# Soft-MoE over thresholded attention on one core: 28 weight blocks are issued pair by pair behind the loads of q, and GpSimd's scaling of k is planned later

## The chip, the cores and the metric

The kernel runs on one core of a Trainium2 chip. A core has five engines with a queue each, which run their instructions in order and wait for each other through semaphores: TensorE (PE in the profile; its weight loads are PEld), VectorE (DVE), ScalarE (ACT), GpSimd (POOL) and SyncE (SP), which here only issues DMA transfers. PE writes to PSUM, GpSimd works on SBUF alone. The metric is the time of one execution on the device in microseconds (us), the median of several runs.

## The reference, cut to what matters

```python
scores = q @ k.T / sqrt(64)                      # 8 batches x 8 heads, 576 x 576, head size 64
thresh = scores.max(-1) - tau
scores = where(scores >= thresh, scores, -1e9)
attn   = softmax(scores);  x = attn @ v          # x: 4608 rows x 512 (all heads of a row side by side)
logits = x @ phi                                 # 32 slots, 4 for each of 8 experts
d = softmax of logits over the 4608 rows;  slot_input = d.T @ x
for e in range(8):                               # w1[e]: 512 x 1024, w2[e]: 1024 x 512
    slot_out[e] = relu(slot_input[e] @ w1[e]) @ w2[e]
out = (softmax of logits over the 32 slots) @ slot_out
```

All of it is computed in 32-bit floats. The weights w1 and w2 are 32 MB; they are needed only after the last attention row is there, since `slot_input` sums over all rows.

## The kernel before, in words

**Pairs.** The attention runs over 32 pairs of heads, `NP` = 8 batches x 4 (`pair(p)`, line 448). A pair loads its k (two transfers, L468), its q (two transfers, one for each head's 64 partitions, L473) and its v (one, L480). Two buffers each for k, q and v are there, so a pair's k and q can be loaded only when the pair before the last has made all its scores, and v when that pair has multiplied by its v. The k is first multiplied by a flag over 8 (L475): by VectorE in halves for the first pair, by GpSimd in one instruction of 128 x 576 for every other.

A pair has nine tiles of scores, each 128 x 576: both heads' rows against their keys. For each tile PE makes the scores (L494, the ninth L499), VectorE takes the maximum of a row (L504, `nmx`), ScalarE the exponential (L512), GpSimd works out the threshold (L515, `thr`), and VectorE masks and sums (L518). GpSimd adds a small number to the sums (L525, `ri`), VectorE takes the reciprocal (L528), and GpSimd normalises the tile, called `p` or `pL` (L532). Then PE transposes (L420), ScalarE copies the transposes out of PSUM (L425 and L564; `pTa`, `pTb`, `pTl`), PE multiplies by v (L579) and transposes back. After each fourth pair the batch's logits, its running softmax over rows and its share of `slot_input` are made (`dispatch`, line 622).

PSUM holds four regions, each for one tile of scores or a set of transposes. The tail after the last pair (lines 810 to 971) runs the experts and the combination.

**The weights.** The 64 blocks of 512 KB (a block is 128 x 1024) are fetched by `load_unit` (L397; the transfer for w1 is L404, for w2 L406). The first `NPRE` = 28 go to buffers of their own, which are free from the beginning; 19 more, called `host`, go after the last loads of the attention into room that the attention gives back, and the last 17 in the tail.

**The order of the work** is made while the program is built, by a list planner (`Order`, line 99). `G.add(engine, duration, number, function, reads, writes, after)` registers an operation. `plan` (line 150) walks through a modelled time: an operation becomes ready when all it depends on has ended, plus a latency of the engine it comes from, `LAT` (or `SAME` where the same engine follows). A free engine takes, among the ready operations that find a buffer, the one with the lowest number. The numbers are in steps, nine to a pair, and most are replaced by those in `TABLE` (lines 34 to 79), which are kept by pair and by the operation's place in it. `after` adds a dependence for the planner alone. The planned times set the order in each engine's queue and the buffers, nothing else; on the chip each instruction then waits for the data and buffers that it needs. For a transfer SP's `LAT` is the time that the planner allows from the end of the issue to the landing.

In the table the loads of k and GpSimd's scaling of k have low numbers (39 and 19 steps ahead of their pair), so that each is taken as soon as it is ready.

For the changed lines: in `pair`, the loads and the scaling; after the loop over the pairs, the loop that registers the 28 blocks, with numbers 8, 12, 16 and so on up to 116 and no dependence:

```python
for i in range(NPRE):
    G.scope("load", 4 * (i + 2))
    G.add("SP", 1460, 4 * (i + 2), lambda i=i: load_unit(wslots[i]))
```

Of the kernel before, what the change touches and what calls it, by code (L numbers as in the profile page):

```python
# [14 lines left out]
AX = mybir.AxisListType  # L15
PSUM = bass.MemoryType.PSUM

LAT = {"PE": 197, "DVE": 140, "ACT": 152, "POOL": 160, "SP": 2400}
SAME = {"PE": 0, "DVE": 127, "ACT": 143, "POOL": 0, "SP": 2100}
SLOTS = dict(  # L20
    k=2, q=2, vv=2, r=3, ri=3, nmx=4, thr=4, p2=4, pL=1, pTa=1, pTb=1, pTl=1, l4=1,
# [77 lines left out]
class Order:  # L99
# [50 lines left out]
    def plan(self, table):  # L150
# [49 lines left out]
        while ev:  # L200
# [10 lines left out]
            for eng in engs:  # L211
# [26 lines left out]
                heapq.heappush(ev, (end, 2, -1))  # L238
                heapq.heappush(ev, (end + LAT[eng], 0, got))
                for j in succ[got]:  # L240
                    left[j] -= 1
                    lat = (SAME if ops[j][0] == eng else LAT)[eng]
                    rdy[j] = max(rdy[j], end + lat)
# [24 lines left out]
def softmax_attention_soft_moe(  # L268
# [17 lines left out]
    nc = tc.nc  # L286
    B, HP, D, _, S = qT.shape
    NP = B * HP
    N9 = 9
# [87 lines left out]
    G = Order(kinds)  # L377
# [10 lines left out]
    wslots = [wp.tile([128, 1024], F32, name=f"w{i}") for i in range(NPRE)]  # L388
# [3 lines left out]
    n = NPRE + NHOST  # L392
# [4 lines left out]
    def load_unit(t):  # L397

        if len(where) == len(units):
            return  # L400
        i, kind, _, e, k = units[len(where)]
        where[i] = t
        if kind == 0:
            nc.sync.dma_start(t, w1[e, k * 128:(k + 1) * 128, :])  # L404
        else:
            nc.sync.dma_start(t, w2[e, k * 256:(k + 1) * 256, :].rearrange("(p j) f -> p (j f)", j=2))  # L406
# [41 lines left out]
    def pair(p):  # L448
        b, j = divmod(p, HP)
        t0 = p * N9  # L450
        G.scope("first" if p == 0 else "last" if p == NP - 1 else "pair", t0)
        kt, qt, vv = (Buf(k) for k in ("k", "q", "vv"))
# [5 lines left out]
        def pool(dur, nom, fn, r, w):  # L458
            G.add("POOL", dur, nom, fn, r, w)
# [4 lines left out]
        for hs in parts:  # L464
            kc, n = slice(hs[0] * HS, (hs[-1] + 1) * HS), len(hs)
            def keys(a=hs[0], z=hs[-1] + 1):
                for g in range(2):
                    nc.sync.dma_start(  # L468
                        kt.t[rows[g]].rearrange("p (h k) -> p h k", h=2)[:, a:z],
                        kT[b, j, :, 0:2 * S].rearrange("d (h g k) -> d g h k", h=2, g=2)[:, g, a:z])  # L470
            G.add("SP", 1200, t0 - 18 + hs[0], keys, w=[kt[h] for h in hs])
            for g in range(2):
                G.add("SP", 500 * n, t0 - 18 + hs[0], lambda g=g, a=hs[0], z=hs[-1] + 1: nc.sync.dma_start(  # L473
                    qt.t[rows[g], a:z], qT[b, j, :, a:z]), w=[qt[h, g] for h in hs])
            sc = lambda e, kc=kc: lambda: e.tensor_scalar(out=kt.t[:, kc], in0=kt.t[:, kc], scalar1=flag8, **one)  # L475
            if p == 0:
                G.add("DVE", 370, t0 - 9 + hs[0], sc(nc.vector), [], [kt[h] for h in hs])
            else:
                pool(730, t0 - 9, sc(nc.gpsimd), [], [kt[h] for h in hs])
        G.add("SP", 1100, t0 - 12, lambda: nc.sync.dma_start(vv.t, vt[b, j]), w=[vv], after=vload[-1:])  # L480
        vload.append(len(G.ops) - 1)

        p2s = {}
        for i in range(N9):
            t = t0 + i
            s, nmx, thr = Buf("s"), Buf("nmx"), Buf("thr")
            c, h = divmod(i, 2)
# [44 lines left out]
            if i < 8 and h == 1:  # L534
                w = Buf("s")
# [8 lines left out]
            if i == 3:  # L544
                w = Buf("s")
# [7 lines left out]
            if i == 8:  # L553


                w = Buf("s")
# [12 lines left out]
        for a, (pT, q) in enumerate(((pTa, slice(0, QA)), (pTb, slice(QA, S)))):  # L569
            n0 = u + OFF['a1' if a else 'a0']  # L570
            w = Buf("w")
            n = q.stop - q.start
# [12 lines left out]
        w = Buf("s")  # L585
# [148 lines left out]
    def csoft(rows):  # L734
# [7 lines left out]
        def guard():  # L742
# [10 lines left out]
    G.scope("load", 0)  # L753
    G.add("SP", 200, -12, lambda: nc.sync.dma_start(phi_sb, phi.rearrange("(j p) s -> p j s", p=128)),
          w=[PERS["phi"]])
    recent, last, vload = [], [], []
    for p in range(NP):
        recent.append(len(G.ops))
        pair(p)
        if p % HP == HP - 1:  # L760
            dispatch(p // HP)
    for i in range(NPRE):
        G.scope("load", 4 * (i + 2))
        G.add("SP", 1460, 4 * (i + 2), lambda i=i: load_unit(wslots[i]))

    G.scope("soft", NP * N9)
    for eng, n, fn in csoft(slice(0, row(B - 1))):
# [30 lines left out]
    for i in range(NHOST):  # L798
        n = next(n for n in range(NL) if sum(x[1] for x in sides[:n + 1]) >= (i + 1) * 4096)
        G.add("SP", 1350, NP * N9 + 9, lambda n=n, i=i: host(NL - 1 - n, i),  # L800
              after=sorted(set(sum(users[:n + 1], []))))
# [217 lines left out]
```

## Time and profile before

| what | value |
|---|---|
| median of three runs | 618.53 us (618.26 to 618.58) |
| the profiled execution | 613.17 us, of which 611.4 us span from the first to the last instruction |
| mean granted TensorE clock of the profiled execution | 0.977 |
| busy share of the span | PE 90%, VectorE 80%, ScalarE 72%, GpSimd 57% |
| moved by DMA | 82.98 MB, mean 136 GB/s |
| weight blocks (`w<-in_w`) | 45 of 512 KB, median 9.4 us from issue to landing |

How to read it: the profile is of one execution. A row of a timeline has the start and the length in us, the engine, the line of the kernel, the operation, what it writes and reads, the shape and how many were merged; in square brackets stand the idle time of the engine just before it and what ended that. A `q` behind an engine's name marks its queue's own instructions, such as the issue of a transfer. A row of a group has the busy time, the mean length in nanoseconds, and behind the second bar the idle time before the group and what ended most of it. A row of a table by stage has the busy time of each engine with its number of instructions, then the granted clock, the share of the 16 DMA engines that was busy, and GB/s. The issues are listed with their number, the size and the median us to landing. Idle time before an instruction that "ended" with an engine means that this engine's signal was the last that came.

The median of the runs is 5.36 us above the profiled execution.

### The profile page before, as it was taken

The page shows a single profiled execution, that of the slowest core. Times are in us where ns is not written, and L with a number is a line of the kernel's source. Part 1 is how long each engine was busy: PE and PEld are TensorE (multiplying, and loading weights), DVE is VectorE, ACT ScalarE, POOL GpSimd, SP SyncE. Part 2 cuts the span into 40 slices and gives each one's busy share as a digit, 9 for nine tenths or more (in the row PEclk, how much of TensorE's full clock was granted, in tenths as well). Part 3 has the DMA queues.
Part 4 walks back from the last instruction along what each step waited for, and adds up shares of the span by engine and source line. Part 5 has one row for each costly group of instructions (what it writes and reads, how often), then busy time and mean ns, then how long its engine had stood idle before and what let it go on. Part 6 is the DMA issues. An engine that isn't in the chain of part 4 may idle for free.

```text
span 611.4 us, 17335 instructions
## 1 busy us (share of the span) xinstructions
PE 547.4 (90%) x6342; PEld 332.8 (54%) x6342; DVE 487.1 (80%) x1146; ACT 442.5 (72%) x751; POOL 350.5 (57%) x799
## 2 busy tenths in 40 slices
PE   7799899999999999998999899899999998889991
PEld 5455555555555555555555555555565555443361
DVE  5689888898998988998898888898989999341182
ACT  3588878788888888888878788788788888512071
POOL 2666666666666765666656665676667746311030
PEclk9599999999999999999999999999999999989997
DMA  7989943133322332333333232233223321799578
GB/s 194 271 273 342 317 109 83 36 84 83 85 71 62 88 80 64 83 81 80 82 81 81 81 81 67 61 81 82 70 69 82 80 60 58 265 359 374 209 297 322
DMA packets 31989, 82.98 MB, mean 136 GB/s; under 512 B 4640, under 2 KB 12832, under 8 KB 31904
## 3 DMA queue, kind: packets, MB, share of 16 engines
q1 hardware_dynamic: 31904, 81.87, 43.9%
q8 instruction: 50, 0.82, 0.6%
q14 instruction: 35, 0.29, 0.2%
HBM read 72.42 MB, written 9.44 MB: 134 GB/s over the span
## 4 chain that ended last, share of the span: by engine, by line
PE 54%; ACT 16%; DVE 13%; issue 10%; POOL 3%; DMA 1%; DVEq 0%; SPq 0%; POOLq 0%; ACTq 0%
PE ps L579 18%; PE ps L494 13%; PE ps L420 10%; ACT p L512 8%; DVE p L518 6%; DVE nmx L504 4%; PE ps L499 3%; PE h L857 3%; ACT pTa L425 2%; PE so L887 2%; ACT pTl L425 2%; POOL p L532 2%; ACT pTb L425 1%; PE o L922 1%; PE ps L713 1%
## 5 line engine op out<-in xcount | busy, mean ns | idle before, releaser
L504 DVE TENSOR_REDUCE nmx<-ps 128x1 f32<-128x576 f32 x288 | 205.3, 752 | 33.4 <-PE ps L494 29.5
L518 DVE SCALAR_TENSOR_TENSOR p<-ps,thr,p 128x576 f32<-128x576 f32 x256 | 199.8, 812 | 9.2 <-POOL thr L515 7.7
L512 ACT ACTIVATE p<-ps,nmx 128x576 f32<-128x576 f32 x256 | 183.4, 746 | 30.3 <-DVE nmx L504 25.8
L532 POOL TENSOR_SCALAR p<-p,ri 128x576 f32<-128x576 f32 x256 | 189.4, 745 | 11.1 <-PE ps L420 3.1
L494 PE MATMUL ps<-k,q 64*128 64x288 f32 x1024 | 171.8, 438 | 6.7 <-issue 3.0
L420 PE MATMUL ps<-ident,p 64*128 64x64 f32 x2304 | 110.1, 229 | 24.8 <-ACT pTl L425 9.2
L420 PEld LDWEIGHTS ps<-ident,p 64*128 64x128 f32 x2304 | 90.9, 140 | 57.7 <-DVE p L518 15.5
L494 PEld LDWEIGHTS ps<-k,q 64*128 64x128 f32 x1024 | 86.8, 190 | 40.5 <-ACT pTb L425 11.4
L515 POOL TENSOR_SCALAR thr<-nmx,nabs 128x1 f32<-128x1 f32 x288 | 75.7, 268 | 34.0 <-DVE nmx L504 28.1
L525 POOL TENSOR_SCALAR ri<-r 128x2 f32<-128x2 f32 (+1 forms) x160 | 30.9, 193 | 98.7 <-DVE ri L528 43.5
L425 ACT COPY pTb<-ps 128x1024 f32<-128x1024 f32 (+1 forms) x95 | 80.8, 878 | 2.3 <-PE ps L420 1.3
L579 PE MATMUL ps<-pTb,vv 128*64 128x320 f32 x512 | 75.9, 438 | 0.3
L425 ACT COPY pTa<-ps 128x1024 f32<-128x1024 f32 x64 | 65.4, 1024 | 11.7 <-PE ps L420 11.0
L579 PE MATMUL ps<-pTa,vv 128*64 128x256 f32 x512 | 62.6, 387 | 0.0
L425 ACT COPY xT<-ps 128x256 f32<-128x256 f32 (+1 forms) x63 | 25.2, 400 | 51.1 <-PE ps L579 51.1
L579 PEld LDWEIGHTS ps<-pTb,vv 128*64 128x64 f32 x512 | 34.0, 136 | 37.1 <-ACT pTb L425 11.4
L579 PEld LDWEIGHTS ps<-pTa,vv 128*64 128x64 f32 x512 | 34.1, 137 | 26.3 <-ACT pTa L425 11.5
L475 POOL TENSOR_SCALAR k<-k,flag 128x576 f32<-128x576 f32 x31 | 23.0, 743 | 34.8 <-DMA k<-in_kT 21.2
L579 PE MATMUL ps<-pTl,vv 128*64 128x256 f32 (+1 forms) x256 | 41.9, 406 | 0.0
L528 DVE RECIPROCAL ri<-ri 128x2 f32<-128x2 f32 (+1 forms) x160 | 25.8, 161 | 15.1 <-POOL ri L525 15.0
L822 POOL TENSOR_TENSOR c<-lall,crow 128x512 f32<-128x512 f32 x9 | 9.3, 1045 | 46.8 <-PE ct L412 42.2
L425 ACT COPY pTl<-ps 128x256 f32<-128x256 f32 x64 | 23.7, 371 | 11.6 <-DVE p L518 7.8
(119 smaller groups left out, 485.4 us busy)
## 6 DMA issues: line engine op xcount, KB each, us to landing
w<-in_w SPq DMA_DIRECT2D x45, 512.0 KB, 9.4
q<-in_qT SPq DMA_DIRECT2D x62, 288.0 KB, 4.6
vv<-in_vt SPq DMA_DIRECT2D x32, 320.0 KB, 3.0
host<-in_w SPq DMA_DIRECT2D x19, 512.0 KB, 6.0
k<-in_kT SPq DMA_DIRECT2D x62, 144.0 KB, 3.1
out<-w SPq DMA_DIRECT2D x11, 512.0 KB, 5.6
out<-host SPq DMA_DIRECT2D x5, 512.0 KB, 6.4
out<-host SPq DMA_DIRECT2D x4, 256.0 KB, 4.9
```

The lines of the kernel that those rows point to most:

```text
L420: nc.tensor.transpose(out=s[:, g, c:c + 64], in_=ins[g], identity=ident[rows[g], rows[g]], tile_position=(64 * g, 0))
L425: G.add("ACT", 51 + 0.833 * n, nom, lambda: nc.scalar.copy(*io()), r, w)
L475: sc = lambda e, kc=kc: lambda: e.tensor_scalar(out=kt.t[:, kc], in0=kt.t[:, kc], scalar1=flag8, **one)
L494: nc.tensor.matmul(s.t[:, g, 0:HS], qt.t[rows[g], h, c * 128:(c + 1) * 128], kt.t[rows[g], h * HS:(h + 1) * HS], start=True, stop=True, ti ...
L504: dve(665, t + OFF['mx'], [s], [nmx], lambda s=s, nmx=nmx: nc.vector.tensor_reduce(out=nmx.t, in_=s.t[:, :, 0:HS], axis=AX.XY, op=ALU.max, ...
L512: G.add("ACT", 624, t + OFF['ex'], lambda s=s, nmx=nmx, view=view: nc.scalar.activation(view().rearrange("p (a k) -> p a k", a=2), s.t[:, ...
L515: pool(250, t + OFF['th'], lambda nmx=nmx, thr=thr: nc.gpsimd.tensor_scalar(out=thr.t, in0=nmx.t, scalar1=-1.0, scalar2=nabs, op0=ALU.mult ...
L518: lambda s=s, thr=thr, view=view, i=i: nc.vector.scalar_tensor_tensor(out=view().rearrange("p (a k) -> p a k", a=2), in0=s.t[:, :, 0:HS], ...
L525: pool(200, t + OFF['ri'], lambda e=e: nc.gpsimd.tensor_scalar(out=ri.t[:, e], in0=r.t[:, e], scalar1=1e-9, scalar2=1.0, op0=ALU.add, op1= ...
L528: dve(84, t + OFF['ri'], [], [ri[c]], lambda e=e: nc.vector.reciprocal(ri.t[:, e], ri.t[:, e]))
L532: pool(725, t + OFF['sc'], lambda k=k, view=view_: nc.gpsimd.tensor_scalar(out=view(), in0=view(), scalar1=ri.t[:, k:k + 1], **one), [ri[c ...
L579: nc.tensor.matmul(w.t[h * 64:(h + 1) * 64, 0:n], vv.t[:, v0:v0 + 64], p0, start=(kb == 0), stop=(kb == 4), tile_position=(0, h * 64), ski ...
```

## The change

The changed kernel registers the 28 blocks with a dependence and another number: blocks 0 and 1 come after the second registered load of q of the fourth pair, blocks 2 and 3 after that of the fifth, and so on to the 17th. Their number is the first step of that pair. `qload` keeps the place of that load for each pair. The planner's numbers for SP change too: a transfer is taken to land 4500 ns after its issue (before: 2400), and the issues' durations are 1340 for k (1200), 620 for a load of q (500 for a half, 1000 for a whole one), 450 for v (1100) and 590 for a block of weights (1460). By the rules above GpSimd's scaling of k becomes ready for the planner 1340 + 4500 ns after the start of its load, where it was 1200 + 2400.

No instruction is added or taken away, no buffer and no transfer changes its size, and the arithmetic is the same.

```diff
-LAT = {"PE": 197, "DVE": 140, "ACT": 152, "POOL": 160, "SP": 2400}
+LAT = {"PE": 197, "DVE": 140, "ACT": 152, "POOL": 160, "SP": 4500}
...
-            G.add("SP", 1200, t0 - 18 + hs[0], keys, w=[kt[h] for h in hs])
+            G.add("SP", 1340, t0 - 18 + hs[0], keys, w=[kt[h] for h in hs])
             for g in range(2):
-                G.add("SP", 500 * n, t0 - 18 + hs[0], lambda g=g, a=hs[0], z=hs[-1] + 1: nc.sync.dma_start(
+                G.add("SP", 620, t0 - 18 + hs[0], lambda g=g, a=hs[0], z=hs[-1] + 1: nc.sync.dma_start(
                     qt.t[rows[g], a:z], qT[b, j, :, a:z]), w=[qt[h, g] for h in hs])
...
-        G.add("SP", 1100, t0 - 12, lambda: nc.sync.dma_start(vv.t, vt[b, j]), w=[vv], after=vload[-1:])
+        G.add("SP", 450, t0 - 12, lambda: nc.sync.dma_start(vv.t, vt[b, j]), w=[vv], after=vload[-1:])
         vload.append(len(G.ops) - 1)
+        qload.append(len(G.ops) - 2 - (p > 0))
...
-    recent, last, vload = [], [], []
+    recent, last, vload, qload = [], [], [], []
...
     for i in range(NPRE):
-        G.scope("load", 4 * (i + 2))
-        G.add("SP", 1460, 4 * (i + 2), lambda i=i: load_unit(wslots[i]))
+        G.scope("load", (i // 2 + 3) * N9)
+        G.add("SP", 590, (i // 2 + 3) * N9, lambda i=i: load_unit(wslots[i]), after=[qload[i // 2 + 3]])
```

## The prediction

> **What bounds the kernel now.** I read the page first, for the engines, then a table by stage, then the groups and waits of the long middle, then the timelines of single pairs and of the first 35 us.
>
> ```profile
> span 611.4 us, 17335 instructions
> PE 547.4 (90%) x6342; PEld 332.8 (54%) x6342; DVE 487.1 (80%) x1146; ACT 442.5 (72%) x751; POOL 350.5 (57%) x799
> ...
> core 0: us, PE busy (x) PEld busy (x) DVE busy (x) ACT busy (x) POOL busy (x), PEclk, DMA share, GB/s
> 6.00:30.00 24.00, 17.04 (x121) 10.68 (x121) 17.29 (x40) 11.79 (x16) 12.17 (x28) 0.64 1.00 263
> 12.70:29.70 17.00, 12.18 (x88) 7.49 (x90) 11.91 (x30) 8.76 (x13) 10.03 (x22) 0.50 1.04 276
> 124.00:188.00 64.00, 59.99 (x752) 37.13 (x748) 57.09 (x137) 52.87 (x90) 44.31 (x100) 1.00 0.32 82
> ```
>
> By shares of the span TensorE seems to bound and GpSimd (POOL) to be idle almost half the time. The stage rows say more. In a full stretch (124 to 188) PE and VectorE are both near 90% busy and the DMA engines a third. From 6 to 30 us the DMA engines are full, PE has half its clock, and VectorE is idle for 24.00 - 17.29 = 6.7 us; the later stretch would leave it 6.91 x 24 / 64 = 2.6 us of the same length. So the start has 4.1 us of idle time too many.
>
> In the middle the question is what VectorE waits for. These are the groups from 60 to 510 us; after the last bar stand the idle time before the group and what ended it.
>
> ```profile
> L518 DVE SCALAR_TENSOR_TENSOR p<-ps,thr,p 128x576 f32<-128x576 f32 x223 | 173.8, 812 | 8.7 <-POOL thr L515 7.5 <-ACT p L512 0.8
> L475 POOL TENSOR_SCALAR k<-k,flag 128x576 f32<-128x576 f32 x28 | 20.8, 743 | 30.3 <-DMA k<-in_kT 20.8 <-PE ps L494 7.8 <-PE ps L656 1.6
> ```
>
> POOL stands idle before the scaling of k 30.3 us in 28 pairs, 1.1 us each; most of it ends with the landing of k. VectorE's masking step (L518) lost 7.5 us to the threshold that POOL makes (L515) and 0.8 to ScalarE. Do these belong together? Two pairs side by side, POOL and VectorE in each, and of the second the issue of its k and the matmuls whose later four are the first to read it:
>
> ```profile
> 348.43 0.74 POOL L475 TENSOR_SCALAR k<-k,flag 128x576 f32<-128x576 f32 x1 [2.24 <-DMA k<-in_kT]
> 349.89 0.52 POOL L515 TENSOR_SCALAR thr<-nmx,nabs 128x1 f32<-128x1 f32 x2
> 350.19 0.82 DVE L518 SCALAR_TENSOR_TENSOR p<-ps,thr,p 128x576 f32<-128x576 f32 x1 [1.34 <-POOL thr L515]
> ...
> 150.17 1.33 SPq L468 DMA_DIRECT2D k<-in_kT  x2
> 153.74 0.16 DVE L528 RECIPROCAL ri<-ri 128x2 f32<-128x2 f32 x1
> 154.29 0.74 POOL L475 TENSOR_SCALAR k<-k,flag 128x576 f32<-128x576 f32 x1 [0.93 <-DMA k<-in_kT]
> 155.02 0.74 POOL L532 TENSOR_SCALAR p<-p,ri 128x576 f32<-128x576 f32 x1
> 155.75 0.52 POOL L515 TENSOR_SCALAR thr<-nmx,nabs 128x1 f32<-128x1 f32 x2
> 156.05 0.82 DVE L518 SCALAR_TENSOR_TENSOR p<-ps,thr,p 128x576 f32<-128x576 f32 x1
> 164.38 1.31 PE L494 MATMUL ps<-k,q 64*128 64x288 f32 x8
> ```
>
> A wait of 0.93 us is just covered: the first threshold ends at about 156.02, where VectorE comes free. A wait of 2.24 gives a stall of 1.34, that is 2.24 less about 0.9. POOL runs its queue in order, so what stands behind a scaling that waits for k waits too, the thresholds among them, and VectorE waits for these. Does a stall lengthen the pair? The starts of one matmul group of consecutive pairs, and a stall between the last two:
>
> ```profile
> 124.43 1.95 PE L579 MATMUL ps<-pTa,vv 128*64 128x256 f32 x16
> 139.43 1.95 PE L579 MATMUL ps<-pTa,vv 128*64 128x256 f32 x16
> 331.93 1.95 PE L579 MATMUL ps<-pTa,vv 128*64 128x256 f32 x16
> 333.93 0.82 DVE L518 SCALAR_TENSOR_TENSOR p<-ps,thr,p 128x576 f32<-128x576 f32 x1 [0.77 <-ACT p L512]
> 347.62 1.95 PE L579 MATMUL ps<-pTa,vv 128*64 128x256 f32 x16
> ```
>
> The quiet pair takes 15.00 us, the one with a stall of 0.77 takes 15.69: about 0.7 more. A stall goes into the time nearly one for one.
>
> **The start.** SyncE's issues, then the median time to landing of those issued at 11.0, at 17.3, and of all from 130 to 480 us, then what waited:
>
> ```profile
> 9.45 1.53 SPq L404 DMA_DIRECT2D w<-in_w  x3
> 11.03 0.69 SPq L473 DMA_DIRECT2D q<-in_qT  x1
> 17.30 1.35 SPq L468 DMA_DIRECT2D k<-in_kT  x2
> ...
> q<-in_qT SPq DMA_DIRECT2D x1, 288.0 KB, 10.6
> k<-in_kT SPq DMA_DIRECT2D x2, 144.0 KB, 7.2
> q<-in_qT SPq DMA_DIRECT2D x44, 288.0 KB, 4.5
> k<-in_kT SPq DMA_DIRECT2D x44, 144.0 KB, 3.1
> ...
> 21.72 1.42 PE L494 MATMUL ps<-k,q 64*128 64x288 f32 x4 [3.01 <-issue]
> 23.18 0.76 DVE L504 TENSOR_REDUCE nmx<-ps 128x1 f32<-128x576 f32 x1 [3.60 <-PE ps L494]
> 25.55 0.74 POOL L475 TENSOR_SCALAR k<-k,flag 128x576 f32<-128x576 f32 x1 [4.14 <-DMA w<-in_w]
> 26.60 0.17 DVE L528 RECIPROCAL ri<-ri 128x2 f32<-128x2 f32 x1 [1.19 <-POOL ri L525]
> ```
>
> The second half of q for the second pair is issued behind three weight blocks at 11.03 and lands 10.6 later, at 21.6; the scores of that pair start at 21.72, after PE stood still for 3.01 and, behind it, VectorE for 3.60. Then POOL waits 4.14 for the k of the third pair, issued among weights at 17.30, and holds up a reciprocal on VectorE by 1.19. Here the weights are the cause.
>
> **The change, part by part.**
>
> *Weights out of the first 80 us.* The number of transfers stays. Without the three blocks q's second half is issued at about 9.5 and lands, with the usual 4.5 and the loads ahead of it, near 14, before PE is free at 21.72 - 3.01 = 18.7. VectorE's 3.60 falls to the 0.5 or so that it waits for scores in a quiet pair: -3.1. The k of the third pair lands by about 17.3 + 0.7 + 3.1 = 21.1, when POOL gets there (25.55 - 4.14 = 21.4): the 1.19 shrinks to the usual quarter, -0.9, of which PE at half clock takes some back, since the twelve score matmuls at 26.0 lie between. I take 3.5 for the start. Bounds: the excess of 4.1 above, with 0.5 more for the clock; and nothing at all (or -1, a longer wait of the first pair, whose second key half the planner now believes later) if the slow PE sets the pace there.
>
> *Two blocks behind q's loads, in the 4th to 17th pair.* SyncE issues 28 blocks there, and they stand ahead of the next v load.
>
> ```profile
> 43.55 2.67 SPq L404 DMA_DIRECT2D w<-in_w  x5
> SPq L480 <- PE ps L579: 310.7, 28, 13.8
> ```
>
> An issue takes 2.67 / 5 = 0.53 us, two take 1.1; the v load behind them waits 310.7 / 28 = 11.1 us for its buffer anyway, which covers them. The 1.05 MB take 1.05 / 0.263 = 4.0 us at the rate of the start, and the next k is issued some 15 us, a pair, after the last. So nothing; without this cover 1.1 x 14 = 15 us of later v loads, which are used more than a pair later.
>
> *The planner's numbers.* A load of k was ready for it 1200 + 2400 = 3.60 us after its start, and is now at 1340 + 4500 = 5.84. Its priority is far below its neighbours' numbers, so POOL takes it as soon as it believes it landed: 2.24 us later in the queue. In the pair at 154 the k was issued at 150.17 and the scaling could start 4.1 us later; at 5.84 the two normalisations of p and the first thresholds stand ahead of it. The waits, 1.1 in the mean and 2.24 where I looked, go to nothing or a few tenths; thresholds no longer stand behind them, and the 7.5 + 0.8 = 8.3 us of stalls go. The scaled k, ready at 155.03, is first used in the second half of the eight matmuls at 164.38, some 10 us later; it keeps some 7. The same 4500 applies to q and v, whose landing (4.5 us for q) lies as far ahead of their use; their order on PE stays, because the normalised p now comes earlier than before and PE is still in the matmul group ahead of its transposes. What is late next in a pair: nothing new, the 15.0 of the quiet pair. Bounds for this part: 8.3 if all goes, 0 if only the place of the wait changes, -15 if the scaling lands in the worst place (below).
>
> **Sum.** 8.3 + 3.5 = 11.8 us. The profiled execution took 613.17 us with a span of 611.4; it becomes 601.4. The median of the runs, 618.53, is 5.36 above the profiled one; I carry that over as it is: 618.5 - 11.8 = **606.7 us**.
>
> **The clock.** The row from 12.70 to 29.70 has PE at 0.50 while it is busy 12.18 of 17.00. The Trainium skill, "TensorE: Matmul & The Clock Gate", Part 1, says that the gate watches windows of about 3.4 us that run freely, and gives the full clock after one busy window; 17.0 us being five of them, the row agrees. By it a PE without the 3 us hole fills a window earlier.
>
> ```profile
> 26.00 3.20 PE L494 MATMUL ps<-k,q 64*128 64x288 f32 x12
> 42.71 1.73 PE L494 MATMUL ps<-k,q 64*128 64x288 f32 x12
> ```
>
> As a mechanism of this kernel: if the full clock is back before these twelve matmuls of the start, they take 1.73 as later, and 1.5 us more are won: 605.2.
>
> **Rivals.** (1) *Start gains nothing.* PE at half clock sets the pace, and what q no longer delays the slow PE does: 618.5 - 8.3 = 610.2. For it: PE is busy 72% there at half clock; against: the 3.01 hole has q as its end. (2) *The wait only changes place*: the scaling still waits for a later k, or the stalls pass to the normalisations and the transposes behind them; the start alone gains: 615.0. Against: 5.84 exceeds the landing in every row above. (3) *Slower.* The later scaling lands between the normalisations and the first threshold. Priced in the pair at 154: the reciprocal ends at 153.90, two normalisations of 0.74 and the scaling of 0.74 end at about 156.3 with the semaphores, the threshold at 156.6, 0.55 behind VectorE's 156.05. In 27 pairs 14.9 us: 618.5 - 11.8 + 14.9 = 621.6. It decides from 0.44 a pair. Against: with 5.84 the scaling comes at about 150.2 + 5.8 = 156.0, behind the first two thresholds, though by only half a microsecond. (4) *More.* The 5.36 us of the timed runs over the profiled one are longer waits of the same loads: 601.3. Nothing shows it. (5) *No change*: other queues move with the planner's new numbers, and a few tenths lost in each pair eat the 11.8: 618.5.
>
> **Chances.** Forecast 0.47, clock back early 0.10, (1) 0.13, (2) 0.07, (3) 0.10, (4) 0.08, (5) 0.05. Faster by over 0.2% (1.2 us, about what a measurement of this kernel can tell from no change) are the forecast, the clock, (1), (2), (4): 0.85; within it (5): 0.05; slower (3): 0.10. The range from 600.5 to 615.5 holds all but (3) and (5).
>
> **What would show it.** Right: full DMA share gone from the first 80 us and the transfers spread to 260; the idle time before L475 near zero; no stall of L518 on thresholds in the middle; the reduction at 23.18 about 3 us earlier with half a microsecond of idle time. Wrong: quiet pairs longer than 15.0 us, thresholds (L515) ending late behind the scaling, or a first 30 us as long as today.

## The result

| | median, us | runs |
|---|---|---|
| before | 618.39 | 615.59 to 618.58, 4 runs |
| after | 602.81 | 601.39 to 602.94, 4 runs |

The ratio is 0.9753, with a 95% interval from 0.9722 to 0.9784: 15.6 us less. The forecast was 606.7 with a range from 600.5 to 615.5. The profiled execution went from 613.17 to 602.87 us, 10.3 less, and its span from 611.4 to 601.2. So after the change the profiled execution and the median agree to 0.06 us, where they lay 5.36 apart before. Runs over 1.5% above the fastest of the same kernel on their chip are left out of all that follows; before scatters by itself, so this takes away its slow end too (on one chip 9 of 23 runs, which moves its median from 614.0 to 613.1), and it takes E1's profile, so that of its repetition E11 is read.

### The profile after

Lines from 475 on are one higher than before (the masking step L518 is now L519, the threshold L515 is L516, the matmul by v L579 is L580). First the page and the table by stage of the kernel after:

```profile
span 601.2 us, 17348 instructions
PE 545.1 (91%) x6342; PEld 332.0 (55%) x6342; DVE 485.8 (81%) x1146; ACT 442.3 (74%) x751; POOL 350.7 (58%) x799
...
core 0: us, PE busy (x) PEld busy (x) DVE busy (x) ACT busy (x) POOL busy (x), PEclk, DMA share, GB/s
6.00:30.00 24.00, 19.84 (x167) 12.58 (x167) 19.69 (x46) 13.26 (x20) 12.72 (x31) 0.72 0.48 119
13.14:26.79 13.65, 11.85 (x86) 7.19 (x88) 11.31 (x27) 8.21 (x12) 10.06 (x22) 0.50 0.38 89
```

Busy times have hardly moved. In the first 30 us the DMA engines fell from full to 0.48 and VectorE's idle time from 6.7 to 24.00 - 19.69 = 4.3 us; the stretch at half clock is 13.65 us long, where it was 17.

To compare the middle I take the same work in both: from the third pair's matmul by v to the last pair's. The stages, then VectorE's masks and GpSimd's scalings in it, first of before:

```profile
59.33:527.21 467.88, 432.40 (x5360) 266.62 (x5358) 413.48 (x980) 382.47 (x647) 308.27 (x703) 1.00 0.32 87
...
L518 DVE SCALAR_TENSOR_TENSOR p<-ps,thr,p 128x576 f32<-128x576 f32 x231 | 180.1, 812 | 9.0 <-POOL thr L515 7.5 <-ACT p L512 0.8 <-POOL p L532 0.2
```

and of after (the scalings from 60 to 510 us):

```profile
56.55:516.77 460.22, 430.02 (x5361) 265.72 (x5359) 412.16 (x980) 382.25 (x647) 308.51 (x703) 1.00 0.40 108
...
L519 DVE SCALAR_TENSOR_TENSOR p<-ps,thr,p 128x576 f32<-128x576 f32 x231 | 180.1, 812 | 2.9 <-POOL thr L516 2.8
L475 POOL TENSOR_SCALAR k<-k,flag 128x576 f32<-128x576 f32 x27 | 20.1, 743 | 0.0
```

The same 980 VectorE instructions take 467.88 - 460.22 = 7.66 us less. VectorE's idle time falls by (467.88 - 413.48) - (460.22 - 412.16) = 6.34, of which the masks' is 9.0 - 2.9 = 6.1; the other 1.3 are shorter busy times. GpSimd's wait ahead of the scaling, 30.3 us before, is 0.0. The rest of the span: the start (up to the third pair's matmul by v) went from 59.33 to 56.55, 2.8 less, and the tail from 84.2 to 84.4.

A quiet pair of the kernel after on GpSimd, with the place of its scaling:

```profile
134.01 1.47 POOL L533 TENSOR_SCALAR p<-p,ri 128x576 f32<-128x576 f32 x2 [0.71 <-PE ps L495]
135.47 0.52 POOL L516 TENSOR_SCALAR thr<-nmx,nabs 128x1 f32<-128x1 f32 x2
136.14 0.27 POOL L516 TENSOR_SCALAR thr<-nmx,nabs 128x1 f32<-128x1 f32 x1
136.39 0.74 POOL L475 TENSOR_SCALAR k<-k,flag 128x576 f32<-128x576 f32 x1
137.22 0.19 POOL L526 TENSOR_SCALAR ri<-r 128x2 f32<-128x2 f32 x1
```

The scaling starts without a wait, behind two normalisations and three thresholds; none of those can be held up by a late k any more. Over the whole queue it stands 2 to 5 places further back in 29 of 31 pairs. Of the planned operations, PE's and ScalarE's have the same order as before, VectorE's differs in 32 places of 811. And the start, on PE and VectorE:

```profile
19.13 1.40 PE L495 MATMUL ps<-k,q 64*128 64x288 f32 x4 [0.19 <-DVE p L519]
20.56 0.76 DVE L505 TENSOR_REDUCE nmx<-ps 128x1 f32<-128x576 f32 x1 [0.76 <-PE ps L495]
23.39 3.20 PE L495 MATMUL ps<-k,q 64*128 64x288 f32 x12
26.52 2.06 PE L580 MATMUL ps<-pTa,vv 128*64 128x256 f32 x16
```

PE's hole of 3.01 us is 0.19, VectorE's 3.60 is 0.76, and the reduction starts at 20.56 instead of 23.18. The twelve score matmuls still take 3.20.

### The profile page after: what moved, and what is told of

Its sections match the earlier page's. It is cut to its first block, busy times and chain, and to the rows that moved or that the text cites. A ratio compares the mean times of both kernels' runs of the same rounds, so it can differ in the third digit from the quotient of the medians.

```text
span 601.2 us, 17348 instructions
## 1 busy us (share of the span) xinstructions
PE 545.1 (91%) x6342; PEld 332.0 (55%) x6342; DVE 485.8 (81%) x1146; ACT 442.3 (74%) x751; POOL 350.7 (58%) x799
## 4 chain that ended last, share of the span: by engine, by line
PE 55%; ACT 22%; DVE 9%; issue 7%; POOL 4%; DMA 1%; DVEq 0%; POOLq 0%; ACTq 0%
PE ps L580 23%; PE ps L495 10%; PE ps L420 10%; ACT p L513 6%; ACT pTb L425 5%; ACT pTa L425 4%; DVE p L519 4%; ACT pTl L425 3%; PE h L859 3%; PE so L889 2%; DVE nmx L505 2%; POOL p L533 2%; ACT pTl L565 1%; PE ps L714 1%; ACT x L425 1%
## 5 line engine op out<-in xcount | busy, mean ns | idle before, releaser
L513 ACT ACTIVATE p<-ps,nmx 128x576 f32<-128x576 f32 x256 | 183.7, 747 | 30.3 <-DVE nmx L505 25.8
L519 DVE SCALAR_TENSOR_TENSOR p<-ps,thr,p 128x576 f32<-128x576 f32 x256 | 199.7, 812 | 3.1 <-POOL thr L516 2.8
L420 PE MATMUL ps<-ident,p 64*128 64x64 f32 x2304 | 107.0, 229 | 23.3 <-POOL thr L516 9.1
L420 PEld LDWEIGHTS ps<-ident,p 64*128 64x128 f32 x2304 | 89.6, 140 | 54.4 <-POOL thr L516 14.4
L516 POOL TENSOR_SCALAR thr<-nmx,nabs 128x1 f32<-128x1 f32 x288 | 75.9, 267 | 37.0 <-DVE nmx L505 27.6
L580 PE MATMUL ps<-pTb,vv 128*64 128x320 f32 x512 | 75.9, 438 | 1.4
L580 PE MATMUL ps<-pTa,vv 128*64 128x256 f32 x512 | 62.4, 386 | 0.0
L580 PEld LDWEIGHTS ps<-pTb,vv 128*64 128x64 f32 x512 | 34.0, 136 | 39.2 <-ACT pTb L425 13.8
L580 PEld LDWEIGHTS ps<-pTa,vv 128*64 128x64 f32 x512 | 34.0, 137 | 26.3 <-ACT pTa L425 11.5
L580 PE MATMUL ps<-pTl,vv 128*64 128x256 f32 (+1 forms) x256 | 41.9, 406 | 0.0
L425 ACT COPY pTl<-ps 128x256 f32<-128x256 f32 x64 | 23.7, 370 | 6.0 <-PE ps L420 5.8
L519 DVE SCALAR_TENSOR_TENSOR pL<-ps,thr,pL 128x576 f32<-128x576 f32 x32 | 26.0, 814 | 0.7 <-ACT pL L513 0.7
```

The source lines that it names most:

```text
L420: nc.tensor.transpose(out=s[:, g, c:c + 64], in_=ins[g], identity=ident[rows[g], rows[g]], tile_position=(64 * g, 0))
L425: G.add("ACT", 51 + 0.833 * n, nom, lambda: nc.scalar.copy(*io()), r, w)
L513: G.add("ACT", 624, t + OFF['ex'], lambda s=s, nmx=nmx, view=view: nc.scalar.activation(view().rearrange("p (a k) -> p a k", a=2), s.t[:, ...
L516: pool(250, t + OFF['th'], lambda nmx=nmx, thr=thr: nc.gpsimd.tensor_scalar(out=thr.t, in0=nmx.t, scalar1=-1.0, scalar2=nabs, op0=ALU.mult ...
L519: lambda s=s, thr=thr, view=view, i=i: nc.vector.scalar_tensor_tensor(out=view().rearrange("p (a k) -> p a k", a=2), in0=s.t[:, :, 0:HS], ...
L580: nc.tensor.matmul(w.t[h * 64:(h + 1) * 64, 0:n], vv.t[:, v0:v0 + 64], p0, start=(kb == 0), stop=(kb == 4), tile_position=(0, h * 64), ski ...
```

## The experiments

The theory: a late k holds GpSimd, the thresholds behind it are late, VectorE stands; standing behind them, the scaling can wait without harm. The rivals: the gain is the blocks leaving the first 80 us; or it is some other reordering by the new numbers; or the large difference of the medians is a matter of chips and runs. Three groups of kernels ran on three chips, each beside runs of before on its own chip (medians 615.3, 612.6 and 613.1).

For each profiled execution I split the span in three as above: start (to the third pair's matmul by v), middle, tail. All values in us.

| kernel | start | middle | tail | median of runs |
|---|---|---|---|---|
| before, first profile | 59.33 | 467.88 | 84.2 | 618.39 |
| before, second (E4) | 57.33 | 474.37 | 84.3 | 614.2 |
| after, first | 56.55 | 460.22 | 84.4 | 602.81 |
| after, second (E5) | 55.32 | 460.10 | 84.2 | 602.92 |
| after, third (E10) | 56.46 | 460.03 | 84.2 | 602.46 |
| blocks moved alone (E11) | 56.59 | 471.52 | 86.1 | 610.77 |
| the same, with a later scaling (E3) | 57.12 | 462.11 | 86.0 | 606.59 |
| numbers alone (E2) | 57.58 | 462.15 | 84.0 | 608.55 |
| numbers alone (E9) | 58.76 | 461.57 | 84.4 | 609.76 |
| scaling 1 us later (E8) | 56.29 | 461.37 | 86.3 | 605.44 |
| two places mended (E12) | 55.57 | 459.60 | 84.3 | 601.45 |
| scaling earlier (E6) | 59.39 | 501.24 | 84.3 | 645.05 |
| all blocks behind one load (E7) | 55.89 | 483.81 | 84.4 | 626.45 |

### E4, E5, E10: the two kernels again

No edit: before once more (E4), after twice (E5, E10).

> The kernel before, unchanged, to see why its timed runs lie 5.4 us above its profiled execution. If the difference belongs to the measurement, profile and times differ again by about 5 us. If it is another mood of the same waits, a profile with a span near 616 us shows longer waits before L475 or a longer start, and the sum of VectorE's stalls behind thresholds is above 8.3 us.

> The changed kernel unchanged, on one chip with the three runs beside it. My theory: with the scaling behind the latest landing its time no longer depends on when k lands, so its runs lie within some 3 us of each other (the kernel before spread over 9 us, 611.3 to 620.4, in the last comparison) around 603 to 605 us, 10 to 13 us below the kernel before. If the spread belongs to the chip, the changed kernel spreads as widely.

> The changed kernel beside the three others: 601 to 604 us as on the two chips before, whatever the kernel before takes here.

Measured: E4 has ratio 0.9993 (0.9956 to 1.003), its runs from 611.49 to 617.79 in nine; the 19 of before beside it go from 611.33 to 620.35. E5 has 0.9839 (0.9798 to 0.988), 601.39 to 603.15 in six; E10 0.9838 (0.9795 to 0.9881), 601.65 to 603.41 in six. So after is within 2.0 us in 16 runs on several chips, with middles that agree to 0.2 us, and before scatters over 9 us on one chip; on the chip of E10 its fastest run took 605.82. On the chips of E5 and E10 the medians lie 9.7 and 10.6 us apart, near the 10.3 of the first two profiles and not the 15.6 of the result: how much the change wins depends on how slow before happens to run. Two profiles of the unchanged kernel before differ in both parts. The masks and the scalings of E4 from 60 to 510 us:

```profile
L518 DVE SCALAR_TENSOR_TENSOR p<-ps,thr,p 128x576 f32<-128x576 f32 x219 | 170.8, 813 | 12.2 <-POOL thr L515 11.7
L475 POOL TENSOR_SCALAR k<-k,flag 128x576 f32<-128x576 f32 x28 | 20.7, 740 | 33.2 <-DMA k<-in_kT 25.0 <-PE ps L494 3.9 <-PE ps L656 1.5
```

The scaling's waits are 33.2 us instead of 30.3, and the masks' 12.2 instead of 8.7. One of its late pairs, on SyncE, GpSimd, VectorE and PE:

```profile
277.90 1.33 SPq L468 DMA_DIRECT2D k<-in_kT  x2
282.52 1.95 PE L579 MATMUL ps<-pTa,vv 128*64 128x256 f32 x16
283.83 0.74 POOL L475 TENSOR_SCALAR k<-k,flag 128x576 f32<-128x576 f32 x1 [2.74 <-DMA k<-in_kT]
285.59 0.82 DVE L518 SCALAR_TENSOR_TENSOR p<-ps,thr,p 128x576 f32<-128x576 f32 x1 [1.83 <-POOL thr L515]
302.02 1.95 PE L579 MATMUL ps<-pTa,vv 128*64 128x256 f32 x16
```

The scaling could start at 283.83, 5.9 us after the first issue of its k; GpSimd waited 2.74, the mask 1.83: 0.9 less, as the prediction read it. The pair took 302.02 - 282.52 = 19.50 us, though, where its like in after takes 16.1 to 16.2. 1.83 us of stall do not explain 3.3. The table by stage, in windows of 3.4 us, shows what came on top:

```profile
284.05:287.46 3.41, 1.76 (x30) 1.06 (x28) 1.87 (x5) 1.15 (x3) 2.90 (x7) 1.00 0.01 4
287.46:290.87 3.41, 3.41 (x30) 1.75 (x28) 1.83 (x6) 2.66 (x6) 2.25 (x5) 0.50 0.00 0
```

With VectorE standing, PE was busy for only 1.76 of 3.41 us, and the next 3.41 us ran at half clock. In their middles E4 has this twice (again from 389.86), E11 once, E6 below four times, the profiles of after never. Not every such stall brings it: E4's masks also stood 1.82 us until 140.73 and until 352.29, PE was busy for 2.40 and 2.47 us in the window that begins there, and the full clock stayed. So a wait that is 2 us longer than what the thresholds can bear costs the stall, and where it empties one window far enough some 1.5 us of clock on top. The Trainium skill, "TensorE: Matmul & The Clock Gate", Part 1, puts the half clock behind at least one idle window of about 3.4 us; the length agrees here (3.41), but PE was not idle in the window before, it was half busy, so the measurement goes further than the rule.

This makes it likely that the 5.36 us between before's profile and its median were longer waits of this kind, which go with the change. It is not shown: those executions have no profile. What E4 shows is one such execution. By E4 against the first profile: masks +3.5, two windows at half clock about +3, start -2.0, in sum 4.5; the spans differ by 616.0 - 611.4 = 4.6.

### E1 and E11: the blocks moved, the old numbers

Against the kernel after, shortened to the numbers:

```diff
-LAT = {... "SP": 4500}
+LAT = {... "SP": 2400}
...
-    G.add("SP", 1340 (k), 620 (q), 450 (v), ...)
+    G.add("SP", 1200 (k), 500 * n (q), 1100 (v), ...)
```

> Only the loop over the 28 blocks is changed; the planner's numbers for SP stay as before (2400 and the old durations), so the scaling of k keeps its place except in the first pairs. My theory (two separate causes): the start is won, the middle is not. The scores of the second pair start near 19.1 us instead of 21.7, as after the change, 2.7 us; the stalls of VectorE behind thresholds stay in the middle, about 6 to 8 us of them. Profiled span 607 to 609 us (before 611.4, after 601.2). Rival (the transfers themselves, not the place of the scaling, make the difference in the middle): the waits before L475 shrink by themselves and the span comes to 603 or less.

> Again only the loop over the blocks, beside the changed kernel. My theory: 2 to 5 us below the kernel before, 7 to 12 us above the changed kernel, and a spread of several us between runs, since the late landings of k still meet the old place. Rival (with the blocks out of the way k lands early enough): within 3 us of the changed kernel.

Measured: E1 612.91, ratio 0.9943 (0.9902 to 0.9984), nine runs; E11, on another chip, 610.77, ratio 0.9965 (0.9929 to 1.0), twelve runs. The profile is of E11's slowest run. The groups from 60 to 510 us:

```profile
L519 DVE SCALAR_TENSOR_TENSOR p<-ps,thr,p 128x576 f32<-128x576 f32 x221 | 172.3, 812 | 10.6 <-POOL thr L516 10.4
L475 POOL TENSOR_SCALAR k<-k,flag 128x576 f32<-128x576 f32 x27 | 20.0, 739 | 31.9 <-DMA k<-in_kT 21.8 <-PE ps L495 5.8 <-PE ps L657 2.5
```

The start is that of after (56.59), the middle has all its stalls, and more of them than before's first profile (the masks' 10.6 us against 8.7). The blocks bring the start alone: by the two ratios 0.57% and 0.35%, 3.5 and 2.1 us.

### E3: the place of the scaling alone

E1's kernel; once the order is planned, the scaling's planned start is set 2.4 us later, which moves it 1 to 5 places back in GpSimd's queue. PE's, ScalarE's and VectorE's queues stay as they are.

```diff
+        for i, o in enumerate(self.ops):
+            if o[0] == "POOL" and o[1] == 730 and self.noms[i][0] == "pair":
+                start[i] += 2400
         self.start = start
```

> The blocks as after the change, the planner's numbers as before, and GpSimd's scaling of k alone is recorded 2400 planned ns later, 2 to 5 places back in GpSimd's queue; every other instruction of VectorE, TensorE and ScalarE stands as before. My theory: the place of the scaling is all that counts in the middle, so this is as fast as the changed kernel: span 600 to 602 us, waits before L475 below 2 us in all. Rival (the 32 places on VectorE and the 105 on GpSimd that the new numbers move beside the scaling bring the gain): span as in the run with the weights alone, 607 or more.

Measured: 606.59, ratio 0.9836 (0.9758 to 0.9913), against 612.91 of E1 on the same chip: 6.3 less for the place alone. E3's slowest of four runs (607.35) is below E1's fastest of nine (607.49). The same groups (lines three higher):

```profile
L522 DVE SCALAR_TENSOR_TENSOR p<-ps,thr,p 128x576 f32<-128x576 f32 x226 | 177.8, 812 | 3.2 <-POOL thr L519 2.3 <-POOL p L536 0.2
L478 POOL TENSOR_SCALAR k<-k,flag 128x576 f32<-128x576 f32 x27 | 20.0, 739 | 0.0
```

The scaling's waits are gone and the masks' idle time is 3.2; the middle of 462.11 is 9.4 below that of E11's run and 5.8 below that of before's first profile. This separates the theory from "some other reordering": nothing but the scaling moved. I had expected a span of 600 to 602; it is 605.2. About 1.5 of that is a longer stretch at half clock in the tail, about 2 are the pairs around a dispatch, 17.55 to 17.75 instead of 17.25 to 17.43: since after differs from E3 there by the other new places in the queues, these are worth about as much.

### E2 and E9: the new numbers, the old blocks

E1's edit turned round: the kernel before with 4500, 1340, 620 and 450.

> Only the planner's numbers for SP are changed; the 28 blocks go out in the first 80 us as before. My theory: the middle is won, the start is not. VectorE's stalls behind thresholds fall from 8 us to about 2, the scores of the second pair still start near 21.7 us behind q; the k of the pairs 3 to 6 lands 5 to 7 us after its issue, and the later place covers most of that. Span 602.5 to 604.5 us. Rival (weights are the main cause): the span stays above 607.

> Again only the planner's numbers, blocks early, now beside the changed kernel on one chip. My theory: the blocks of the first 80 us let k of the fourth and fifth pair land 9 to 10 us after its issue, later than even the new place, 3 to 4 us in all (16.46 and 16.97 us in two pairs that should take 14.97, in the last such profile); so this is 3 to 5 us slower than the changed kernel. Rival (the blocks cost nothing once the scaling stands later): within 1 us of it.

Measured: E2 608.55, ratio 0.9887 (0.9811 to 0.9963), four runs; E9 609.76, ratio 0.9955 (0.9919 to 0.999), twelve runs from 606.59 to 613.29. The profile of E9 is of its fastest run; its groups from 60 to 510 us:

```profile
L518 DVE SCALAR_TENSOR_TENSOR p<-ps,thr,p 128x576 f32<-128x576 f32 x228 | 177.7, 812 | 2.8 <-POOL thr L515 2.7
L475 POOL TENSOR_SCALAR k<-k,flag 128x576 f32<-128x576 f32 x28 | 20.7, 740 | 2.7 <-DMA k<-in_kT 2.7
```

The middle is as good as after's to 1.4 us. What is left is in the first 80 us, where the blocks still go; here the k of the fifth pair, from its issue on:

```profile
54.08 1.35 SPq L468 DMA_DIRECT2D k<-in_kT  x2
63.67 0.74 POOL L475 TENSOR_SCALAR k<-k,flag 128x576 f32<-128x576 f32 x1 [2.67 <-DMA k<-in_kT]
64.72 0.17 DVE L528 RECIPROCAL ri<-ri 128x2 f32<-128x2 f32 x1 [2.44 <-POOL ri L525]
```

Among blocks, k is there 9.6 us after its first issue, where the numbers allow 5.84; now GpSimd's `ri` stands behind it, and VectorE's reciprocal waits 2.44. From the second pair's matmul by v to the third's and on to the fourth's it took 16.17 and 16.50 us (after, in E10: 14.96 and 14.97): 2.7 lost. Whether the two parts need each other is not shown: on the chip of E9, E10 and E11 the numbers alone win 0.45%, the blocks alone 0.35%, both 1.62%, twice the sum; but on the chip of E1 and E2 the parts win 0.57% and 1.13%, in sum about what both win elsewhere. What remains open: E9's median is 7.3 above after's, its profiled run 4.2; the rest lies in executions of which there is no profile.

### E6: the scaling earlier

In the kernel after:

```diff
-LAT = {... "SP": 4500}
+LAT = {... "SP": 1200}
```

> As the changed kernel, but the planner believes a load of k landed 1200 ns after its issue instead of 4500: the scaling stands one place ahead of its place before, in front of the reciprocal's first step (L525 before). My theory: GpSimd waits 2 to 4 us for k in nearly each pair and holds up the reciprocal, the normalisations and the thresholds; VectorE loses 1 to 3 us in nearly each of 28 pairs, and the time is 25 to 60 us above the kernel before. Rival (the wait on GpSimd is mostly idle time that costs nothing): within 5 us of the kernel before.

Measured: 645.05, ratio 1.0523 (1.0469 to 1.0576). The reciprocal of after (60 to 510 us), then the groups of E6 from 60 to 500 us:

```profile
L529 DVE RECIPROCAL ri<-ri 128x2 f32<-128x2 f32 (+1 forms) x142 | 23.0, 162 | 12.6 <-POOL ri L526 12.5
...
L529 DVE RECIPROCAL ri<-ri 128x2 f32<-128x2 f32 (+1 forms) x127 | 20.6, 162 | 44.7 <-POOL ri L526 44.7
L475 POOL TENSOR_SCALAR k<-k,flag 128x576 f32<-128x576 f32 x25 | 18.6, 743 | 65.5 <-DMA k<-in_kT 61.1 <-PE ps L420 2.5 <-PE ps L495 1.9
```

In most pairs the scaling moved to one place ahead of where before has it, in front of the `ri` step. GpSimd's waits double to 65.5, and the reciprocal, which waits 12.6 us in after, waits 44.7: 32 us more, and the middle is 501.24 - 471.52 = 29.7 longer than E11's. Four windows at half clock fall into it, some 6 of the 30 us if each costs 1.5 as in E4. A few other steps of GpSimd and VectorE moved too, so not all of it need be the one place; but the 32 us stand right behind it: the cost of the wait is set by what stands next behind it.

### E8 and E12: further back, and two places by hand

E8 sets the scaling 1 us later with E3's edit in the kernel after (`+= 1000`). E12 moves, at the same place in the kernel after, one normalisation of the pairs 10, 18 and 26 (counted from 0) behind two thresholds, and the next scalings by 0.8 us:

```diff
+        for i, (name, k, base, _) in enumerate(self.noms):
+            if name == "pair":
+                start[i] += 1000 * ((k, base // 9) in ((18, 10), (18, 18), (18, 26)))
+                start[i] += 800 * ((k, base // 9) in ((3, 11), (3, 19), (3, 27)))
```

> As the changed kernel, but the scaling of k is recorded another 1000 planned ns later, one or two places back in GpSimd's queue; nothing else moves. My theory: in the pairs beside a dispatch the scaling stands in front of the reciprocal's first step or a threshold (0.56 us in three pairs, 0.26 in two others), and this gives back 1 to 2.5 us: 0.998 of the changed kernel's time. If the scaling then delays something else, the same or 1 us slower.

> As the changed kernel, but in the pairs 11, 19 and 27 (the pair behind an odd batch's dispatch begins with the next) one normalisation of p is recorded behind two thresholds instead of in front of them, and there the scaling of k behind one threshold. My theory: the stalls of 0.55 and 0.25 us that VectorE has there behind thresholds go, up to 2.4 us in three places, 600 to 602 us. If the transposes that need this normalisation come later by as much, no difference.

After still has stalls of about 0.55 us in six pairs. One of them, GpSimd and VectorE of after in pair 10:

```profile
170.31 2.19 POOL L533 TENSOR_SCALAR p<-p,ri 128x576 f32<-128x576 f32 x3
172.80 0.82 DVE L519 SCALAR_TENSOR_TENSOR p<-ps,thr,p 128x576 f32<-128x576 f32 x1 [0.55 <-POOL thr L516]
```

Three normalisations in a row stand ahead of a threshold. With E8 the scaling lands in front of another one there:

```profile
168.21 0.75 POOL L478 TENSOR_SCALAR k<-k,flag 128x576 f32<-128x576 f32 x1
168.93 0.27 POOL L519 TENSOR_SCALAR thr<-nmx,nabs 128x1 f32<-128x1 f32 x1
169.23 0.82 DVE L522 SCALAR_TENSOR_TENSOR p<-ps,thr,p 128x576 f32<-128x576 f32 x1 [0.67 <-POOL thr L519]
```

E8: 605.44, ratio 0.9876 (0.9838 to 0.9915), 2.5 us slower than after on its chip (602.92), where I had expected a gain. These pairs went from 17.41 to 17.83, the middle from 460.10 to 461.37; the reciprocal's 0.56 turned into 0.32 twice. Beside that the profile has a start 1.0 longer and, with a window at half clock ahead of it, a tail 2.1 longer than E5's; why these came is open. E12: 601.45, ratio 0.9827 (0.9783 to 0.9871), against 602.46 of E10; the three pairs went from 17.41 to 17.26, the stall from 0.55 to 0.33. It beats before, but its runs (601.02 to 603.0) overlap after's (601.65 to 603.41): not told apart. So after's places are near the best that moving the scaling alone can give.

### E7: all 28 blocks behind one load

In the kernel after:

```diff
-        G.scope("load", (i // 2 + 3) * N9)
-        G.add("SP", 590, (i // 2 + 3) * N9, lambda i=i: load_unit(wslots[i]), after=[qload[i // 2 + 3]])
+        G.scope("load", 3 * N9)
+        G.add("SP", 590, 3 * N9, lambda i=i: load_unit(wslots[i]), after=[qload[3]])
```

> As the changed kernel, but all 28 blocks go out in a row behind q's loads of the fourth pair; only SyncE's queue differs. My theory: spreading is worth only what the late k of the next three or four pairs costs: k lands 6 to 10 us after its issue there, 1 to 3 us behind the scaling's place, 3 to 6 us in all, and the start is as in the changed kernel. Rival (what counts is that the start is free of weights): no more than 1 us above the changed kernel.

Measured: 626.45, ratio 1.0226 (1.0177 to 1.0275). Only SyncE's queue differs from after. SyncE, then who waited:

```profile
38.98 19.65 SPq L404 DMA_DIRECT2D w<-in_w  x19
60.21 1.90 SPq L468 DMA_DIRECT2D k<-in_kT  x2
71.75 0.74 POOL L475 TENSOR_SCALAR k<-k,flag 128x576 f32<-128x576 f32 x1 [14.19 <-DMA k<-in_kT]
72.80 0.17 DVE L529 RECIPROCAL ri<-ri 128x2 f32<-128x2 f32 x1 [13.46 <-POOL ri L526]
73.92 0.49 SPq L473 DMA_DIRECT2D q<-in_qT  x1
87.88 1.42 PE L495 MATMUL ps<-k,q 64*128 64x288 f32 x4 [7.30 <-issue]
```

I had expected 3 to 6 us; one pair took 38.70 instead of 14.97, 23.7 more. What I had left out is SyncE itself: nineteen issues in a row took 19.65 us, 1.03 each, twice the 0.53 of a short row. The k stood behind them, the q behind all 28, and PE then waited for q a second time. With two blocks to a pair this price is not there: the pairs with blocks and those without take the same 14.97 or 14.98.

## Why the prediction was right, and where it was off

- **GpSimd's wait, the late threshold, VectorE's stall.** Right, and shown: the place alone removes the stalls (E3), in E6, with the scaling mostly one place the other way, the middle is 30 us longer, and the stall is the wait less 0.9 in E4 too. 8.3 us was the term for the middle; the same work took 7.66 less in the first pair of profiles, since stalls of 2.9 us stay. The slack of the scaled k, forecast at some 7 us, is 7.74. The scaling stands behind three thresholds rather than two.
- **The start.** 3.5 us was taken, 2.8 was measured in the first pair of profiles (2.6 up to the first pair's matmul by v, 29.13 to 26.52). The mechanism is right for that execution, but the hole is not in every one: in E4 the same half of q, issued at 11.03 behind the same three blocks, took 7.7 us to land instead of 10.6, its scores began at 19.47 with no hole, and the first pair stood at 26.86. So the start is worth about 2 to 3 us in some executions and less in others (E4's third pair stood 0.8 us later than after's first).
- **Two blocks behind q cost nothing.** Right with two to a pair; E7 shows the point from which it isn't.
- **The sum against the profiled execution.** 11.8 forecast, 10.3 measured: 1.5 too much, the 0.7 and 0.6 above and 0.2 in the tail.
- **What failed** is the last step: "the median of the runs, 618.53, is 5.36 above the profiled one; I carry that over as it is". After the change the gap was 0.06. That is the bulk of the miss: 5.36 that did not stay, less 1.5 that was not won, is the 3.9 by which 606.7 lies too high. The step gave no reason; what the gap was made of is argued from E4, not shown. The rival "More" has the mechanism that E4 speaks for (longer waits of the same loads) and a time of 601.3, and was put down with "Nothing shows it". The waits themselves pointed to it: 0.93 in one pair and 2.24 in another of one execution, with a threshold near 0.9 below which they cost nothing, so an execution with landings a microsecond later would cost several microseconds more.
- **The rivals.** "Start gains nothing" holds in part for executions like E4's. "The wait only changes place" doesn't: 0.0 us in 27 pairs. "Slower" is what E8 shows on a small scale where the scaling stands ahead of a threshold. "Clock back early" didn't happen in the first profile: the twelve matmuls took 3.20 as before; in E5 they took 2.84. The half clock itself did end one window of 3.41 us sooner (13.65 us instead of 17), in both kernels behind the first window with PE busy throughout (26.33 to 29.75 before, 23.38 to 26.79 after).

## What to carry to other kernels

An operation that waits for a transfer belongs, in an in-order queue, behind the short steps that another engine is waiting for, if its own first use leaves the room: here 1 to 5 places back won 6.3 us of the median (E3), and with mostly one place forward the middle was 30 us longer (E6). Still further back it can stand ahead of the next such step (E8). If the runs of a kernel scatter more than those of its neighbours, look for a wait that costs nothing up to some length, and something beyond it, before you carry the gap between profile and median over into a forecast. Large transfers that are needed late go out a few at a time behind the small ones that are needed soon: in one row they hold the issuing engine too.

## What the runs showed of the hardware that I had not expected

- One window of 3.4 us in which PE was busy for about half (1.76 of 3.41 us in E4, 1.59 of 3.42 in E11) was followed by a window at half clock, in the middle of a stretch at full clock. Others were not (1.97 of 3.41 in before from 384.74, 1.69 of 3.41 in E6 from 233.88), so what decides is open.
- The landing of a small load under a light load of the DMA engines is not constant, and not by chance alone. From the first issue to the landing of both halves of k it takes 3.9 to 4.1 us in the median of each of eleven profiles of seven different orders (all but E1, E6 and E7), but over 4.6 and up to 6.0 in 3 to 7 of 26 pairs, and these are mostly the same pairs: counted from 0, pairs 22 and 24 in all eleven, 5, 9 and 18 in eight or nine. So it hangs on which k is read or on that place of the program; which, no run here tells.
- An issue of a 512 KB block takes SyncE 0.53 us, and 1.03 us in a row of nineteen.
- Before's median differed with chip and time (618.4, 615.3, 612.6, 613.1) while after's stayed between 602.46 and 602.92. Why is open; what is shown is that the waits through which a late k reaches the end are gone in the three profiles of after.
